# A jump-table hint on TensorE, and earlier loads, tables and drain, in an attention and mixture-of-experts kernel

## The chip, the cores and the metric

The kernel runs on one core of a Trainium2 chip. The core has five engines that work in parallel, each with an instruction stream of its own: TensorE (PE in the profile; its weight loads are listed as PEld), VectorE (DVE), ScalarE (ACT), GpSimd (POOL) and SyncE (SP), which here only issues DMAs. They wait for each other through semaphores. [...] The metric is the device time of one execution in microseconds, as a median over runs.

## The reference

All in float32: talking-heads attention, then a mixture of eight experts of which each token takes one.

```python
def _attn_ref(q, k, v, w_pre, w_post):          # 8 batches, 12 heads, 448 positions, 64 wide
    scores = scale * np.matmul(q, k.transpose(0, 1, 3, 2))
    scores = np.einsum('bhij,hg->bgij', scores, w_pre)
    scores = scores - np.max(scores, axis=-1, keepdims=True)
    attn = np.exp(scores)
    attn = attn / (np.sum(attn, axis=-1, keepdims=True) + 1e-09)
    attn = np.einsum('bhij,hg->bgij', attn, w_post)
    return np.matmul(attn, v)
...
def _moe_ref(x, w_gate, w1, w2):                # 3584 tokens of 768, 8 experts, hidden 1024
    ...
    expert_idx = np.argmax(logits, axis=1)
    ...
    for e in range(E):
        mask = expert_idx == e
        h = np.maximum(x[mask] @ w1[e], 0.0)
        out[mask] = gate_w[mask, None] * (h @ w2[e])
```

## The kernel before

**Attention** takes 32 query tiles (four to a batch: three of 120 queries and one of 88), and cuts each tile into *units* of 20 queries: six for a full tile, five for a short one, 184 in all. A hand-written schedule hangs steps on unit numbers, `at(u, priority, step, ...)`, and emits them unit by unit in order of priority; each engine then executes its own part in that order. The steps that matter here are these. `load_q` brings a tile's queries into `qr`, and `order_q` (POOL, L123) copies them in another order into `qq`, in two halves. `qk` (L238) makes the scores of one pair of heads, beginning QLEAD = 8 units ahead of the tile's own first unit, one pair per unit; a copy on ACT or DVE (L240) takes them out of PSUM, and a relayout DMA (L251) turns them into `sb`. Mixing over heads follows on PE (L265), the maximum on DVE, the exponential on ACT, the weights `wp` on POOL (L290), the second mixing and transposition on PE (L308), a copy `pt` on DVE (L319), and the product with `vt` on PE (L339). `load_k` and `load_v` bring the next batch's keys and values in chunks, and batch 0's values during the first units. At the very start PE warms up on matmuls whose result nobody uses (`heat`), VectorE clears the five `sb` tiles (L190), and small weights arrive through ScalarE's queue.

**Routing** is spread over the attention: for each tile `choose` finds the best expert, `weight` its gate, `count` its place in the expert's list by two small matmuls (L463, L466), and `dispatch` writes token number and gate into the DRAM table `TB` by an indirect DMA on POOL (L485); `store_x` writes the tile's rows into the DRAM array `XD`. The last two tiles (O and T in the code) have a `tail` list of their own that orders these steps by hand, with a long `heat` in it.

**Experts** come after that, one after the other. `load_t` reads 512 entries of an expert's table (L678), a copy `ti` and its clipped form `tcl` follow on DVE (L681, L682), and `load_x` gathers the rows in four slots of 128 tokens by indirect DMAs on POOL (L689). `turn_x` transposes them on PE (L706) and splits them into `xh` and `xl` (float32 precision is kept by splitting each operand into a high and a low part and adding three products). `hidden_of(e)` is a `tc.Switch` on `width[e]`, an entry of the small table `wide` that is known only at run time: it has six bodies, which compute the hidden layer for 352, 384, ... 512 tokens (L770 on PE); the Switch's own instructions are recorded on L951, and each body begins with a hint for the branch at its end (L781). `result(e, s)` makes one slot's output (L797 on PE, L802 on DVE, L804 on ACT, a scatter on POOL at L806); the fourth slot stands in a `tc.If` on the width (L834), since many experts have no more than 384 tokens. The weight chunks are fetched with SP as `wraw` (L519) and split on ACT and DVE (L526, L527). Every engine loads the eight widths into registers (L726). After the last expert a loop serves tokens that did not fit; with these inputs it is not entered, and the program ends with drains and semaphores, recorded on L951.

## Time and profile before

| | |
|---|---|
| time, median of 3 runs | 1334.51 us (1333.62 to 1341.18) |
| the profiled execution | 1335.38 us, span 1333.7 us |
| busy share of the span | PE 92%, VectorE 57%, ScalarE 49%, GpSimd 28% |
| granted TensorE clock, mean | 0.978 of full speed |
| experts begin (first L770 matmul) | 785.70 us |

The trace belongs to one execution; all times in it count from the start of its span. A row of the timeline gives start, length, engine, line, operation, and in brackets how long the engine had stood idle before it and what released it. The releaser is inferred. "issue" means that the profile shows nothing that the engine waited for. Names ending in q, such as PEldq or SPq, are an engine's sequencer or queue: branches, register loads, semaphores and DMA issues, which are not counted as busy. [...]

### The profile page before, as it was taken

To read this page: it belongs to the slowest core of one execution; us is meant where nothing else is said; L and a number is where in the kernel's file an instruction comes from. 1 tells how busy PE (TensorE), PEld (TensorE's weight loads), DVE (VectorE), ACT (ScalarE), POOL (GpSimd) and SP (SyncE) were. 2 spreads that over 40 slices of the span, in tenths; PEclk is the share of its full clock that TensorE was granted. 3 is DMA by queue.
4 is the path that set the end of the run, shared out by engine and by line. 5 is a ranking of instruction groups with operands and counts; after the bars stand their busy time and mean duration, and the time that the engine had idled before them with its cause. 6 is when DMAs were issued, how large, how long until landed. Compare 5 with 4: busy or idle time off the path is not lost. (4 is left out here: it accounts for less than half of the span.)

```text
span 1333.7 us, 54843 instructions
## 1 busy us (share of the span) xinstructions
PE 1223.8 (92%) x23808; PEld 1070.3 (80%) x23808; DVE 754.2 (57%) x1600; ACT 653.2 (49%) x1417; POOL 378.3 (28%) x921
## 2 busy tenths in 40 slices
PE   7789989999999899999999879899999999989995
PEld 3477878777777787877888779798989999979995
DVE  4567767777777677776878555252434243434320
ACT  3466766666666666766775334232323232323220
POOL 2234443435344434344443230101020202010000
PEclk9899999999999999999999979899999999989998
DMA  5655555656565646565645255343444444444210
GB/s 150 174 168 176 179 167 171 189 160 199 163 189 164 183 149 190 156 188 169 182 152 184 67 195 163 123 144 131 144 132 141 145 129 156 155 132 145 86 38 32
DMA packets 116293, 202.08 MB, mean 152 GB/s; under 512 B 40658, under 2 KB 90018, under 8 KB 115924
## 3 DMA queue, kind: packets, MB, share of 16 engines
q1 hardware_dynamic: 108398, 172.16, 42.2%
q0 software_dynamic: 6064, 23.86, 5.2%
q8 instruction: 212, 3.47, 1.1%
q10 hardware_dynamic: 1462, 1.30, 0.4%
q14 instruction: 157, 1.29, 0.3%
HBM read 97.59 MB, written 23.06 MB: 90 GB/s over the span
## 5 line engine op out<-in xcount | busy, mean ns | idle before, releaser
L265 PE MATMUL bm<-sb,Wpre 64*64 64x448 f32 x1440 | 319.5, 546 | 5.2 <-ACT et L277 3.1
L339 PEld LDWEIGHTS bx<-pt,vt 64*64 64x64 f32 x5856 | 282.9, 134 | 23.4 <-issue 11.6
L339 PE MATMUL bx<-pt,vt 64*64 64x120 f32 (+3 forms) x5856 | 290.8, 249 | 8.9 <-issue 4.9
L277 ACT ACTIVATE et<-bm,st 128x448 f32<-128x448 f32 (+1 forms) x368 | 233.0, 636 | 110.0 <-DVE st L271 102.8
L271 DVE TENSOR_REDUCE st<-bm 128x1 f32<-128x448 f32 (+1 forms) x368 | 223.0, 619 | 82.4 <-PE bm L265 65.4
L308 PE MATMUL bp<-wp,et 60*64 60x60 f32 x10080 | 225.5, 223 | 33.1 <-issue 27.3
L308 PEld LDWEIGHTS bp<-wp,et 60*64 60x64 f32 x10080 | 202.5, 136 | 46.6 <-issue 38.6
L319 DVE COPY pt<-bp 128x960 f32<-128x960 f32 (+1 forms) x184 | 215.7, 1172 | 38.8 <-PE bp L308 33.3
L240 ACT COPY si<-bs 120x896 f32<-120x896 f32 (+1 forms) x188 | 170.1, 905 | 102.2 <-PE bs L238 90.9
L238 PE MATMUL bs<-kr,qq 64*64 64x448 f32 x1504 | 194.5, 556 | 7.2 <-ACT si L240 6.9
L290 POOL TENSOR_SCALAR wp<-Wpost,st 128x60 f32<-128x60 f32 (+1 forms) x368 | 110.5, 312 | 239.5 <-DVE st L287 174.8
L265 PEld LDWEIGHTS bm<-sb,Wpre 64*64 64x64 f32 x1440 | 95.5, 135 | 78.9 <-issue 37.9
L770 PE MATMUL pm_h<-xh,ah 128*128 128x512 f32 (+4 forms) x384 | 145.1, 378 | 14.9 <-issue 9.7
L806 POOL DMA_INDIRECT out<-y,ti x30 | 30.9, 1029 | 443.8 <-ACT ah L526 135.7
L770 PE MATMUL pm_h<-xl,ah 128*128 128x512 f32 (+4 forms) x384 | 144.1, 375 | 0.0
L770 PE MATMUL pm_h<-xh,al 128*128 128x512 f32 (+4 forms) x384 | 143.8, 374 | 0.0
L774 DVE SCALAR_TENSOR_TENSOR hl<-pm_h,hh 128x512 fp32r<-128x512 f32 (+4 forms) x64 | 41.0, 641 | 165.5 <-ACT hh L773 164.4
L773 ACT ACTIVATE hh<-pm_h 128x512 fp32r<-128x512 f32 (+4 forms) x64 | 35.7, 558 | 184.5 <-PE pm_h L770 184.5
L797 PE MATMUL pm_y<-bh,hh 128*128 128x384 f32 x480 | 124.7, 341 | 0.0
L797 PE MATMUL pm_y<-bh,hl 128*128 128x384 f32 x480 | 122.3, 336 | 0.0
L797 PE MATMUL pm_y<-bl,hh 128*128 128x384 f32 x480 | 122.3, 336 | 0.0
L804 ACT ACTIVATE y<-pm_y,tb 128x384 f32<-128x384 f32 x30 | 17.4, 580 | 165.2 <-PE pm_y L797 88.2
(123 smaller groups left out, 1616.1 us busy)
## 6 DMA issues: line engine op xcount, KB each, us to landing
sb<-si SPq DMA_DIRECT2D x359, 210.0 KB
wraw<-in_w SPq DMA_DIRECT2D x64, 384.0 KB
wraw<-in_w SPq DMA_DIRECT2D x46, 512.0 KB
vt<-in_v SPq DMA_DIRECT2D x64, 192.0 KB
kr<-in_kT SPq DMA_DIRECT2D x48, 224.0 KB
qr<-in_qT SPq DMA_DIRECT2D x48, 180.0 KB
XD<-xr SPq DMA_DIRECT2D x24, 360.0 KB
qr<-in_qT SPq DMA_DIRECT2D x16, 132.0 KB
```

The lines of the kernel that those rows point to most:

```text
L238: nc.tensor.matmul(out=bank[cs, r, :S], lhsT=QQ[T][hs, c, cs], rhs=KR[b, c][hs, :], start=True, stop=True)
L240: copy(out=SI[T][:ni, 2 * c:2 * c + 2, :], in_=bank[:ni, :, :S])
L265: nc.tensor.matmul(out=bank_m[x][c * D:(c + 1) * D, :S], lhsT=Wpre[hs, :], rhs=SB[T, s][hs, c, :], start=True, stop=True)
L271: nc.vector.reduce_max(out=st[:top, 0, x:x + 1], in_=bank_m[x][:top, :S], axis=AX.X, negate=True)
L277: nc.scalar.activation(out=et[:top, x, :], in_=bank_m[x][:top, :S], func=AF.Exp, bias=st[:top, 0, x:x + 1], scale=1.0, accum_out=st[:top, ...
L290: nc.gpsimd.tensor_scalar(out=wp[:top, x, :], in0=Wpost[:top], scalar1=st[:top, 2, x:x + 1], scalar2=1.0, op0=ALU.mult, op1=ALU.mult)
L308: nc.tensor.matmul(out=bank_p[g * D:(g + 1) * D, n, o:o + nw], lhsT=et[hs, x, j * D:(j + 1) * D], rhs=wp[hs, x, :], start=True, stop=True)
L319: nc.vector.tensor_copy(out=to, in_=src[:, :2 * nh])
L339: nc.tensor.matmul(out=o, lhsT=VT[b % 2][ks, c, h * D:(h + 1) * D], rhs=i, start=(c == 0), stop=(c == NJ - 1))
L770: nc.tensor.matmul(out=ph[:, :n], lhsT=wx[:, fs], rhs=xx[:, kt, :n], start=(m == 0), stop=(m == 3 * NK1 - 1))
L774: nc.vector.scalar_tensor_tensor(out=hl[:, ft, :n], in0=ph[:, :n], scalar=0.0, in1=hh[:, ft, :n].bitcast(F32), op0=ALU.max, op1=ALU.subtract)
L797: nc.tensor.matmul(out=py[g][:, :384], lhsT=hx[:, kt, ts], rhs=wx[:, g * 384:(g + 1) * 384], start=(n == 0), stop=(n == 3 * NK2 - 1))
```

## The change

The change has five parts. (1) In slot 2 of every expert but the last, ahead of `result(e, 2)`, PE gets a jump-table hint: it loads the next expert's width and names the Switch body that this width selects; the Switch then knows of this hint. Only PE has it. (2) The five `sb` tiles are cleared before the small weights' tiles, not behind them. (3) `load_v` of batch 0 comes two units earlier, `load_k` of batch 1 later, and `order_q` one unit later for every tile from 2 on. (4) In the tail, tile O is weighed, counted and dispatched before the last tile's first half is taken; the second product of the last tile (`whole`) comes later; the warming is 66 long instead of 50, and 4 instead of 2 between the first expert's transposes. The widths are computed, and loaded, right behind the last dispatch, ahead of the weight splits, and the two fetches on ScalarE's queue come behind four splits. (5) In the last expert POOL drains before the conditional fourth slot.

```diff
@@
     heat(10, bank_m[0])
+    sbs = [sb_p.tile([P, 2, S], F32, name=f"sb{n}") for n in range(5)]
+    for t in sbs:
+        nc.vector.memset(t, 0.0)
     w12 = const.tile([P, 2, H], F32, name="w12")
...
-    sbs = [sb_p.tile([P, 2, S], F32, name=f"sb{n}") for n in range(5)]
-    for t in sbs:
-        nc.vector.memset(t, 0.0)
...
-                at(max(u0 - QLEAD - 2 + half, 1), 0.5 + 0.01 * T, order_q, T, half)
+                at(u0 - QLEAD - 1 + half, 0.5 + 0.01 * T, order_q, T, half)
         if it == 0 and b + 1 < B:
-            for c, k in enumerate((1, 3, 4, 8, 9, 12)):
+            for c, k in enumerate((1, 3, 4, 8, 9, 12) if b else (7, 8, 9, 10, 11, 13)):
                 at(u0 + k, 5.6, load_k, b + 1, c)
...
-                    (whole, T, 1, banks_s), (take_a, T, 0, bank_m), (take_b, T, 0, bank_m),
-                    (rows, T, (0, 1, 2), bank_x, 0), (weight, O), (store_x, O),
-                    (take_a, T, 1, banks_s), (take_b, T, 1, banks_s), (count, O),
-                    (rows, T, (3, 4, 5), bank_x, 3 * DW), (dispatch, O),
+                    (weight, O), (count, O), (dispatch, O), (take_a, T, 0, bank_m),
+                    (take_b, T, 0, bank_m), (whole, T, 1, banks_s),
+                    (rows, T, (0, 1, 2), bank_x, 0), (store_x, O),
+                    (take_a, T, 1, banks_s), (take_b, T, 1, banks_s),
+                    (rows, T, (3, 4, 5), bank_x, 3 * DW),
...
-                    (weight, T), (count, T), (heat, 50, bank_m[0]), (dispatch, T),
+                    (weight, T), (count, T), (heat, 66, bank_m[0]), (dispatch, T),
...
-        at(k, 5.65, load_v, 0, (k,))
+        at(max(k - 2, -1), 5.65, load_v, 0, (k,))
...
-        next_w(nc.scalar)
-        next_w(nc.scalar)
-        for n in range(2, NK1 - 1):
+        ...
+        width = [nc.values_load(wide[0:1, e:e + 1], min_val=0, max_val=len(WIDTHS) - 1,
+        ...
+        for n in range(RAWLEAD):
             split_w(n)
+        for n in range(2):
+            fetch_w(nc.scalar)
+        split_w(RAWLEAD)
...
-            heat(2, pm_h.tile([P, CAP], F32, name="pm_h"))
+            heat(4, pm_h.tile([P, CAP], F32, name="pm_h"))
...
+    HINT = {}
+
     def hidden_of(e):
         at0 = dict(turn)
-        for n in tc.Switch(width[e], len(WIDTHS)):
+        for n in tc.Switch(width[e], len(WIDTHS), hint=HINT.pop(e, None)):
...
                 if s == NS - 2:
+                    HINT[e + 1] = tc.switch_hint({mybir.EngineType.PE: width[e + 1]}, len(WIDTHS),
+                                                 label=f"wide{e + 1}")
+
                     def between():
...
             result(e, s, between)
+        if e == NE - 1:
+            nc.gpsimd.drain()
         with tc.If(width[e] > WIDTHS.index(SHORT)):
             result(e, NS - 1)
```

The order of PE's stream in expert 0, around the transposes (`pm_x<-ident,xs`) of slot 2; `pm_y` rows are matmuls of `result`. Before:

```order
L797 MATMUL pm_y<-bh_15672,hh 128x384 x2
L797 MATMUL pm_y<-bl_15673,hh 128x384 x2
L797 MATMUL pm_y<-bh_15672,hl 128x384 x2
L706 MATMUL pm_x<-ident,xs 128x128 x6
L797 MATMUL pm_y<-bh_15658,hh 128x384 x2
L797 MATMUL pm_y<-bl_15659,hh 128x384 x2
L797 MATMUL pm_y<-bh_15658,hl 128x384 x2
L797 MATMUL pm_y<-bh_15660,hh 128x384 x2
```

After, where line numbers from here on are those of the changed kernel (L797 has become L802, L706 has become L724):

```order
L802 MATMUL pm_y<-bl_15695,hh 128x384 x2
L802 MATMUL pm_y<-bh_15694,hl 128x384 x2
L724 MATMUL pm_x<-ident,xs 128x128 x6
L834 SWITCH_STRIDE
L669 TENSOR_LOAD wide
L834 ISA
L834 BRANCH_PREFETCH_HINT
L802 MATMUL pm_y<-bh_15680,hh 128x384 x2
L802 MATMUL pm_y<-bl_15681,hh 128x384 x2
L802 MATMUL pm_y<-bh_15680,hl 128x384 x2
L802 MATMUL pm_y<-bh_15682,hh 128x384 x2
```

Four instructions now stand between the transposes and the first matmuls of `result(0, 2)`; the branch that they concern is that of the next Switch, behind the rest of slot 2 and slot 3.

VectorE's stream at the start of the program (`w` and `warm` are the small weights' tile and the tile with which ScalarE warms up; `si<-bx` are the copies of scores). Before:

```order
L92 MEMSET bp 128x1024
L148 MEMSET w_132 128x24
L154 MEMSET warm 1x1
L178 MEMSET Wpre 128x64
L180 SCALAR_TENSOR_TENSOR Wpre<-w_132,mask 128x60
L184 TENSOR_TENSOR Wpost<-w_132,mask 128x60
L190 MEMSET sb_176 128x896
L190 MEMSET sb_177 128x896
L190 MEMSET sb_178 128x896
L190 MEMSET sb_179 128x896
L190 MEMSET sb_180 128x896
L240 COPY si<-bx 120x896 x4
```

After:

```order
L92 MEMSET bp 128x1024
L149 MEMSET sb_132 128x896
L149 MEMSET sb_133 128x896
L149 MEMSET sb_134 128x896
L149 MEMSET sb_135 128x896
L149 MEMSET sb_136 128x896
L151 MEMSET w_142 128x24
L157 MEMSET warm 1x1
L181 MEMSET Wpre 128x64
L183 SCALAR_TENSOR_TENSOR Wpre<-w_142,mask 128x60
L187 TENSOR_TENSOR Wpost<-w_142,mask 128x60
L240 COPY si<-bx 120x896 x4
```

The five clearings moved from between `Wpost` and the first copies to the front, ahead of the clearing of `w`.

SyncE's stream at the junction of attention and experts (`XD<-xr` are the last tiles' rows, `tb<-TB` the read of expert 0's and then expert 1's table). Before:

```order
L251 DMA sb_179<-si 120x1x448
L413 DMA XD<-xr 120x768 x3
L413 DMA XD<-xr 88x768
L726 TENSOR_LOAD wide x8
L678 DMA tb<-TB 128x4x2
L519 DMA wraw_14450<-in_w 128x768
L519 DMA wraw_14451<-in_w 128x768
L519 DMA wraw_14448<-in_w 128x768
L519 DMA wraw_14449<-in_w 128x768
L678 DMA tb<-TB 128x4x2
```

After:

```order
L251 DMA sb_135<-si 120x1x448
L413 DMA XD<-xr 120x768 x3
L413 DMA XD<-xr 88x768
L696 DMA tb<-TB 128x4x2
L520 DMA wraw_14451<-in_w 128x768
L520 DMA wraw_14452<-in_w 128x768
L520 DMA wraw_14449<-in_w 128x768
L520 DMA wraw_14450<-in_w 128x768
L696 DMA tb<-TB 128x4x2
L669 TENSOR_LOAD wide
```

The eight loads of widths ahead of the first read of the table are gone; one load stands behind the second read, ahead of the first Switch, and each later expert has its own.

## Rows read from the trace of the kernel before

**Rows 1.** The page's busy time by engine: busy us (share of the span), instructions.

```profile
PE 1223.8 (92%) x23808; PEld 1070.3 (80%) x23808; DVE 754.2 (57%) x1600; ACT 653.2 (49%) x1417; POOL 378.3 (28%) x921
```

**Rows 2.** The page's group of hidden matmuls, and the list of waits (total, times, longest).

```profile
L770 PE MATMUL pm_h<-xh,ah 128*128 128x512 f32 (+4 forms) x384 | 145.1, 378 | 14.9 <-issue 9.7
PE pm_h L770 <- issue: 9.7, 2, 4.9
PE pm_h L770 <- ACT y L804: 5.2, 5, 1.3
```

**Rows 3.** Line L951, where the Switch is recorded: PE's branches (ns min/median/max), all, then 905 to 914 us.

```profile
L951 PEldq COMPARE_BRANCH  x16: 321/438/4312, 783.6 to 1280.9; - x16
L951 PEldq COMPARE_BRANCH  x1: 3412/3412/3412, 911.0 to 911.0; - x1
```

**Rows 4.** Line L770 by stretch (us, PE busy, PEld busy, PEclk, DMA share, GB/s), and the chain.

```profile
840.00:900.00 60.00, 35.55 (x144) 28.73 (x144) 0.94 0.35 117
905.00:975.00 70.00, 33.24 (x144) 26.97 (x144) 1.00 0.42 136
1181.17 35.08 PE pm_h L770 x144
```

**Rows 5.** Timeline of the beginning: start us, us, engine, line, operation [idle before].

```profile
9.37 4.57 DVE L190 MEMSET sb<- 128x896 f32 x5
13.86 1.03 DVE L240 COPY si<-bx 120x896 f32<-120x896 f32 x1
14.99 1.76 PE L238 MATMUL bx<-kr,qq 64*64 64x448 f32 x8 [5.10 <-POOL qq L123]
```

**Rows 6.** Timeline of the first tiles, and two stretches (PEclk is the number behind POOL's).

```profile
34.94 0.80 POOL L123 COPY qq<-qr 128x360 f32<-128x360 f32 x1 [3.91 <-DMA qr<-in_qT]
37.46 1.10 PE L308 MATMUL bp<-wp,et 60*64 60x60 f32 x56 [2.85 <-DVE pt L319]
61.78 0.35 PE L339 MATMUL bx<-pt,vt 64*64 64x60 f32 x6 [3.47 <-DMA vt<-in_v]
38.00:42.00 4.00, 4.00 (x88) 2.33 (x82) 1.99 (x4) 2.09 (x5) 0.79 (x3) 0.57 0.26 91
62.00:66.00 4.00, 4.00 (x93) 3.47 (x90) 1.70 (x4) 1.45 (x4) 0.88 (x4) 0.57 0.05 18
```

**Rows 7.** The junction: timeline, register loads by line, and a stretch of both.

```profile
760.49 1.03 POOL L485 DMA_INDIRECT TB<-tg,di  x1 [2.74 <-DMA TB<-tg,di]
762.08 1.23 DVE L527 TENSOR_TENSOR al<-wraw,ah 128x1024 fp32r<-128x1024 f32 x1 [0.25 <-issue]
L726 SPq TENSOR_LOAD <-wide x8: 261/273/487, 763.6 to 766.1; - x8
770.04 0.17 DVE L681 COPY ti<-tb 128x4 int32<-128x4 int32 x1 [4.02 <-DMA tb<-TB]
776.12 1.51 PE L706 MATMUL pm_x<-ident,xs 128*128 128x128 f32 x6 [7.56 <-DMA xs<-XD,tcl]
785.70 0.46 PE L770 MATMUL pm_h<-xh,ah 128*128 128x352 f32 x1
772.00:786.00 14.00, 8.21 (x37) 7.84 (x38) 6.34 (x10) 3.35 (x7) 4.42 (x4) 0.51 0.66 227
```

**Rows 8.** The end: timeline of POOL, and POOL's drains on the program's last line.

```profile
1311.28 0.97 POOL L806 DMA_INDIRECT out<-y,ti  x1 [7.40 <-ACT y L804]
1319.60 0.98 POOL L806 DMA_INDIRECT out<-y,ti  x1 [7.34 <-DVEq _compat.py:109]
L951 POOLq DRAIN  x3: 40/112/7834, 1325.0 to 1333.4; - x3
```

**Rows 9.** POOL's waits for qr, the page's score matmuls, and tile 2's first eight of them.

```profile
POOL qq L123 <- DMA qr<-in_qT: 36.4, 16, 5.1
L238 PE MATMUL bs<-kr,qq 64*64 64x448 f32 x1504 | 194.5, 556 | 7.2 <-ACT si L240 6.9
42.29 0.96 PE L238 MATMUL bs<-kr,qq 64*64 64x448 f32 x8
```

## Prediction

> **What bounds the kernel now.** I read the page's table of busy time first: TensorE (PE) is busy for 92% of the span and nothing else passes 57% [rows 1]. So the end moves only where PE stands still, or where it runs at a lower clock. Four kinds of such places matter for this change, and I looked for each in the view that shows it.

> *The jump into an expert's hidden layer.* The page's group of L770 matmuls carries 14.9 us of idle time ahead of it, of which 9.7 is put down to "issue", that is to nothing the profile can name [rows 2]. The list of waits says that these 9.7 us are two waits, the longer 4.9 [rows 2]; the other 5.2 lie in five shorter ones, the longest 1.3 [rows 2]. The rows of the Switch itself name the cause: PE's COMPARE_BRANCH on L951 (Switch branches and body exits together, 16 of them) takes 321 ns at least, 438 ns in the middle, and up to 4312 ns [rows 3]; one ahead of a short stop took 3412 ns [rows 3]. In five experts PE still has matmuls queued while the branch is out, so only a quarter or so of it shows. In the two that follow a skipped fourth slot, PE's queue is empty first and all of it shows.

> *The clock after such a stop.* The 144 hidden matmuls of a 512-wide expert keep PE busy 33.24 us at a granted clock of 1.00, but 35.55 us from 840 on, behind the first long stop, at 0.94 in that stretch [rows 4], and 35.08 us from 1181.17 on, behind the second [rows 4]. The stops of about 1 us leave no such mark.

> *Beginning.* VectorE clears five sb tiles from 9.37 for 4.57 us, and only then makes the copy si<-bx at 13.86 that frees the bank for which PE idles 5.10 us, until 14.99 [rows 5]. The row names POOL as releaser, but POOL's copy is no later than VectorE's, and VectorE's is what stands behind the clearing.

> *Two stalls in the first tiles, the junction, the end.* PE idles 2.85 us before 37.46 and 3.47 before 61.78; ahead of the first, POOL stood for 3.91 us at its copy qq<-qr, for the DMA; the second waits for vt itself [rows 6]. After each the granted clock of 4 us is 0.57 [rows 6]. At the junction the last table entry is scattered at 760.49, VectorE has the read-back table at 770.04, and PE idles 7.56 us before its first transposes at 776.12; it starts hidden work at 785.70, at a clock of 0.51 over these 14 us [rows 7]. At the end the last scatter starts at 1319.60, and then a POOL DRAIN of up to 7.834 us, starting at the 1325.0 of the first of three, runs nearly to the end of the span [rows 8].

> **The parts and their costs.** The profiled execution took 1335.4 us (span 1333.7 and 1.7 outside), 0.9 more than the median of the three runs.

> *Hint on PE.* Added on PE for seven experts: a stride setting, one register load, one register operation and the hint. A load takes about 0.3 us here (273 ns in the middle on SyncE's row [rows 7]), the rest less. They stand among 0.34-us matmul pairs that are queued ahead of execution, and that queue hides them; with no cover they would cost some 0.5 us x 7 = 3.5. What they should remove: if the branch falls from 3.3-4.3 us to the 0.3-0.44 of the hinted exits, the five short stops go (5.2 us), and of the two long ones (9.7) about 1.0 us each stays, since there the queue is drained and the branch and its register work still follow. That is 12.9 us. The clock then stays up: 35.55 - 33.24 = 2.3 and 35.08 - 33.24 = 1.8, together 4.1. Full effect 17.0. Evidence that a hint on PE works at all: half of the 16 branches are exits of bodies of some 290 PE instructions that carry a hint at their head, and the middle of the 16 is 438 ns [rows 3]. But a hint's place is not free: it stands some 215 instructions before its branch, and I cannot show what happens if both lie in one block of fetched code. I count six of seven sites: **14.6 us** (bounds 0 and 17.0; a loss is a rival).

> *Beginning.* The five clearings now come before the small memsets, so VectorE's copy no longer stands behind them; instead ScalarE's issues and its warm-up come some 4.5 us later, because they wait for a memset behind the clearing. PE's 5.10 us stop could vanish, and ScalarE's first copies slip by about 3 us, which takes part of it back. **3 us** (bounds 0 and 5.1).

> *Early loads.* vt of batch 0 is issued two units earlier, the next batch's kr later, and POOL's copy qq<-qr one unit later, so POOL stands less in front of the weights wp that PE waits for. Prices of the two stalls: 2.85 + 3.47, plus a clock of 0.57 for 4 us twice, 0.43 x 4 x 2 = 3.4; together 9.8. The earlier vt shares the queue with the first relayouts, so I do not take all: **7 us** (bounds 0 and 9.8). Later tiles: POOL waits 36.4 us for qr in all, 16 times [rows 9]; PE's idle time after most of these is small, and I take nothing.

> *Junction.* The last but one tile's table entry goes out before the last tile's work instead of after it, so the last scatter needn't wait for it (it waited 2.74 us [rows 7]); SyncE's eight register loads from 763.6 to 766.1, ahead of its read of the table, are gone [rows 7]. But VectorE now does its eight loads and four weight splits before it looks at the table. Four splits of 1.2 us [rows 7] behind eight loads of 0.3, all behind the widths, which are ready near 759, give about 768.4 with the casts ahead of the first split, instead of 770.04: 1.6. The warming runs 66 long instead of 50, so PE should reach the transposes at a higher clock; what that saves of 776.12 to 785.70 is limited by the gathers. **2.5 us** (bounds -1 and 5).

> *Drain.* POOL drains before the last conditional, in slot 3's matmuls: slot 2's scatter starts 8.3 us before slot 3's [rows 8]. If the 7.83 us are work that has piled up and can be done early, the drain runs from 1312.3 to 1320.1, the last scatter is about 1 us late and the final drain short (the shortest DRAIN there takes 40 ns): 6.7 us saved. If it begins only as late behind the scatter as it did at the end (5.4 us), it delays the last scatter by some 5 us and saves 2.8. If it is a fixed price of the end, nothing is saved. I take **6 us**, nearer to the first.

> Sum: 14.6 + 3 + 7 + 2.5 + 6 = 33.1; 1335.4 - 33.1 = 1302.3, say 1302.

> **Rivals.** *The hint does nothing* (the fetch still begins only at the branch). For it: a one-shot hint through a register is in no row of before. Against: the hinted exits. Time 1302 + 14.6 = 1317. [...]

> *The drain cannot be brought forward*: 1308, or 1307 to 1311 with a late scatter. For it: no row shows a long drain anywhere but at the end.

> *The other side: score matmuls starved by order_q.* POOL's copy for tiles from 2 on moves one unit closer to the matmuls that read it. In tile 2, the tightest, the copy starts at 34.94 and lasts 0.80, and the tile's first score matmul starts at 42.29: 6.5 us [rows 6, 9]. A unit is near 3.8 us (188 groups of eight score matmuls over some 710 us [rows 9]), so 2.7 us remain. From the point where POOL comes 2.7 us later than now, each further us costs 1 us in each of 30 tiles; 1.6 us further is 48 us, which makes 1302 + 48 = 1350. Against: each tile has its own slack, and the longest wait of POOL for qr, 5.1 us [rows 9], shrinks with the move.

> **How the numbers follow.** Forecast with all parts 0.62; hint without effect 0.19 (1317); drain without effect, hint working 0.12 (1308); starved matmuls 0.03 (1350); other small failures together 0.04 (hint and drain both idle, 1323). With every part at its better bound the time would be 1335.4 - 17 - 5.1 - 9.8 - 5 - 6.7 = 1292; I cut this to 1293. On the upper side 1318 takes in the hint that does nothing. Outside are the double failure, the starved matmuls and the tails, under 0.2. A measurement of this kernel can tell about 1% from no change, which puts the bounds at 1321 and 1348. Faster than 1321 are all cases but the last two: 0.88; within 1% the double failure and weak tails, 0.09; slower 0.03.

> **What would show it.** Hint: PE's COMPARE_BRANCH on the Switch line with its maximum below 0.5 us, "issue" ahead of the hidden matmuls from 9.7 to about 2, and 33.2 us for 512-wide experts throughout. If the seven branches stay at 3.3-4.3 the hint failed. Beginning: the 5.10 gone, a stop of at most 2 in its place. Early loads: no stop over 2 us between 25 and 65. Junction: first transposes near 774, minus what came before. Drain: one long DRAIN before the last scatter, short ones at the end, and some 14 minus 6 us from the last matmul to the end. The forecast is wrong above all if hints on PE serve only branches with a fixed target, or if the drain waits for something that ends late anyway.

## The result, and the profile after

| | before | changed |
|---|---|---|
| median, first comparison (4 runs each) | 1337.85 us | 1303.68 us |
| ratio to before, 95% interval | | 0.968 (0.9624 to 0.9737) |
| ratio in a second comparison (6 runs against 11) | | 0.9747 (0.9707 to 0.9786) |
| profiled execution: span, mean granted clock | 1333.7 us, 0.978 | 1303.2 us, 0.995 |

The forecast was 1302. The ratios come from fast runs alone; the medians of the first comparison, which hold one slow run of the changed kernel, give 0.974, and so do those of the second. The span of the profiled pair can be cut at three instructions that both have: PE's last count matmul of routing (L463), the first hidden matmul of the experts (L770, now L773), and the end of the last matmul.

| stretch | before | changed | difference |
|---|---|---|---|
| start to the last count (attention) | 757.0 | 752.6 | -4.4 |
| last count to first hidden matmul (junction) | 28.7 | 27.2 | -1.5 |
| first hidden matmul to the last matmul (experts) | 532.6 | 515.1 | -17.5 |
| last matmul to the end (tail) | 15.4 | 8.3 | -7.1 |

The page's busy row and its clock row of the changed kernel:

```profile
PE 1216.5 (93%) x23852; PEld 1069.6 (82%) x23852; DVE 758.3 (58%) x1600; ACT 654.7 (50%) x1417; POOL 378.6 (29%) x921
PEclk9999999999999999999999999999999999999999
```

PE does the same work (44 matmuls more, all warming) and has fewer idle microseconds around it; no slice of the span lies below nine tenths of the clock. What answers to [rows 2, 3], PE's branches on the Switch line (now L961; ns min/median/max) and the page's group of hidden matmuls:

```profile
L961 PEldq COMPARE_BRANCH  x16: 321/418/3345, 776.6 to 1257.5; - x16
L961 PEldq COMPARE_BRANCH  x1: 2922/2922/2922, 776.6 to 776.6; - x1
L961 PEldq COMPARE_BRANCH  x1: 3345/3345/3345, 968.1 to 968.1; - x1
L961 PEldq COMPARE_BRANCH  x1: 1766/1766/1766, 1103.9 to 1103.9; - x1
L773 PE MATMUL pm_h<-xh,ah 128*128 128x512 f32 (+4 forms) x384 | 143.0, 372 | 5.6 <-issue 3.9
```

Of the seven hinted branches five take 0.32 to 0.34 us, that of expert 5 takes 1.77, that of expert 3 is as long as before. The eighth, of the first expert, has no hint; it took 0.35 us before and takes 2.92 now. The idle time ahead of the hidden matmuls fell from 14.9 to 5.6, and 2.92 of the 5.6 are the first expert's. What answers to [rows 4] (stretch, PE busy, PEld busy, clock, DMA share, GB/s), the two experts behind a skipped slot:

```profile
830.00:890.00 60.00, 33.24 (x144) 26.97 (x144) 1.00 0.45 143
1155.00:1200.00 45.00, 33.24 (x144) 26.97 (x144) 1.00 0.46 147
```

Both 512-wide hidden layers now take the 33.24 us that only the others took. At the beginning and in the first tiles, answering to [rows 5, 6]:

```profile
11.60 1.08 DVE L240 COPY si<-bx 120x896 f32<-120x896 f32 x1
12.22 0.98 PE L238 MATMUL bs<-kr,qq 64*64 64x448 f32 x8 [1.60 <-ACT si L240]
38.00:42.00 4.00, 3.04 (x98) 1.85 (x94) 2.87 (x6) 2.34 (x6) 0.80 (x3) 1.00 0.71 231
62.00:66.00 4.00, 4.00 (x142) 3.66 (x135) 3.27 (x6) 3.18 (x9) 1.74 (x5) 1.00 0.81 227
```

VectorE's copy comes 2.3 us earlier; PE's stop of 5.10 has become one of 1.60, for ScalarE's copy, which now waits for its late start (in the other runs with the early clearings it is longer, as told below). Both stretches that ran at 0.57 run at 1.00. At the junction, answering to [rows 7]:

```profile
754.44 1.03 POOL L485 DMA_INDIRECT TB<-tg,di  x1 [1.59 <-DVE wf L664]
758.69 4.63 DVE L528 TENSOR_TENSOR al<-wraw,ah 128x1024 fp32r<-128x1024 f32 x4 [0.50 <-DMA tb<-TB]
763.24 0.16 DVE L699 COPY ti<-tb 128x4 int32<-128x4 int32 x1
769.95 0.85 PE L724 MATMUL pm_x<-ident,xs 128*128 128x128 f32 x6 [2.24 <-DMA xs<-XD,tcl]
779.78 0.40 PE L773 MATMUL pm_h<-xh,ah 128*128 128x352 f32 x1 [2.92 <-issue]
767.00:780.00 13.00, 6.80 (x56) 6.11 (x55) 6.49 (x20) 3.45 (x8) 3.47 (x3) 1.00 0.54 180
```

The table is in VectorE's hands 10.7 us behind the last count instead of 13.1; the row shows that VectorE takes it the moment that its four splits end. The clock stays at 1.00. Then 2.92 us are lost ahead of the first hidden matmul. At the end, answering to [rows 8], two scatters and the drains (L843 is the new one, L961 the program's end):

```profile
1287.87 0.98 POOL L811 DMA_INDIRECT out<-y,ti  x1 [7.40 <-ACT y L809]
1297.60 0.98 POOL L811 DMA_INDIRECT out<-y,ti  x1 [8.75 <-issue]
L843 POOLq DRAIN  x1: 8968/8968/8968, 1287.7 to 1287.7; - x1
L961 POOLq DRAIN  x3: 46/113/140, 1301.2 to 1302.9; - x3
```

The record of the new drain begins under the scatter ahead of it (to 1288.85) and goes on for 7.8 us, the length of the drain at the end of before. The last three take 0.3 us together. The last scatter begins 2.8 us behind VectorE's part of `y` (1294.80) instead of 1.4.

### The profile page after: what moved, and what is told of

The parts are those of the page before. It is cut to its first block, busy times and chain, and to the rows that moved or that the text cites. A ratio compares the mean times of both kernels' runs of the same rounds, so it can differ in the third digit from the quotient of the medians.

```text
span 1303.2 us, 54974 instructions
## 1 busy us (share of the span) xinstructions
PE 1216.5 (93%) x23852; PEld 1069.6 (82%) x23852; DVE 758.3 (58%) x1600; ACT 654.7 (50%) x1417; POOL 378.6 (29%) x921
## 3 DMA queue, kind: packets, MB, share of 16 engines
q14 instruction: 155, 1.27, 0.3%
## 5 line engine op out<-in xcount | busy, mean ns | idle before, releaser
L238 PE MATMUL bs<-kr,qq 64*64 64x448 f32 (+1 forms) x1504 | 195.1, 547 | 13.2 <-ACT si L240 10.3
L773 PE MATMUL pm_h<-xh,ah 128*128 128x512 f32 (+4 forms) x384 | 143.0, 372 | 5.6 <-issue 3.9
L773 PE MATMUL pm_h<-xl,ah 128*128 128x512 f32 (+4 forms) x384 | 142.5, 371 | 0.0
L773 PE MATMUL pm_h<-xh,al 128*128 128x512 f32 (+4 forms) x384 | 142.0, 370 | 0.0
L802 PE MATMUL pm_y<-bh,hh 128*128 128x384 f32 x480 | 124.6, 341 | 0.0
L802 PE MATMUL pm_y<-bh,hl 128*128 128x384 f32 x480 | 122.4, 336 | 0.0
L802 PE MATMUL pm_y<-bl,hh 128*128 128x384 f32 x480 | 122.3, 336 | 0.0
L809 ACT ACTIVATE y<-pm_y,tb 128x384 f32<-128x384 f32 x30 | 17.5, 582 | 165.0 <-PE pm_y L802 81.1
```

Source lines behind the costliest of these rows:

```text
L238: nc.tensor.matmul(out=bank[cs, r, :S], lhsT=QQ[T][hs, c, cs], rhs=KR[b, c][hs, :], start=True, stop=True)
L773: nc.tensor.matmul(out=ph[:, :n], lhsT=wx[:, fs], rhs=xx[:, kt, :n], start=(m == 0), stop=(m == 3 * NK1 - 1))
L802: nc.tensor.matmul(out=py[g][:, :384], lhsT=hx[:, kt, ts], rhs=wx[:, g * 384:(g + 1) * 384], start=(n == 0), stop=(n == 3 * NK2 - 1))
```

## The experiments

**Without the hint.**

```diff
                 if s == NS - 2:
-                    HINT[e + 1] = tc.switch_hint({mybir.EngineType.PE: width[e + 1]}, len(WIDTHS),
-                                                 label=f"wide{e + 1}")
-
                     def between():
```

> The changed kernel without the hint; everything else as changed. If the hint is what shortened the experts, PE's seven Switch branches from the second expert on are back at 3.3 to 4.3 us, the two stops behind skipped slots at 4.8 to 4.9 us, the 512-wide experts behind them at 35 us instead of 33.2, and the stretch from the first to the last matmul of the experts is 16 to 18 us longer than in the changed kernel (515 us there, 532 before): about 1319 in all. Rival: the experts got shorter by the new order of weight fetches and register loads; then that stretch stays within 4 us of 515 and the time near 1304.

1328.97 us, ratio 0.9899 (0.9852 to 0.9946), clear of both intervals of the changed kernel. The experts take 534.2 us, 19.1 more than with the hint. The Switch line (here L958), the waits, the chain, and the hidden layer behind the first skipped slot by stretch:

```profile
L958 PEldq COMPARE_BRANCH  x16: 322/425/4897, 783.8 to 1281.4; - x16
PE pm_h L773 <- issue: 10.6, 2, 5.9
PE pm_h L773 <- ACT y L809: 7.0, 5, 1.6
1181.39 35.24 PE pm_h L773 x144
836.00:890.00 54.00, 34.81 (x144) 28.16 (x144) 0.97 0.37 117
```

All that [rows 2 to 4] show is back, the loss of clock somewhat smaller in the first of the two layers (34.81 us instead of 35.55), so the rival (that the new order of weight fetches shortened the experts) falls.

**The hint alone**, in the kernel before: `HINT` and the `hint=` of the Switch as in the change, nothing else.

```diff
-        for n in tc.Switch(width[e], len(WIDTHS)):
+        for n in tc.Switch(width[e], len(WIDTHS), hint=HINT.pop(e, None)):
...
+                    HINT[e + 1] = tc.switch_hint({mybir.EngineType.PE: width[e + 1]}, len(WIDTHS),
+                                                 label=f"wide{e + 1}")
```

> The kernel before with the hint alone. By the forecast's mechanism 13 to 17 us less than before (1318 to 1322 where before is 1335), all of it in the experts; the first matmul of the experts near 785.7 as before. One or two of the seven branches may stay long, where no boundary of fetched code lies between hint and branch. Rival: hint and the other parts only work together; then less than 6 us.

Ratio 0.9854 (0.9812 to 0.9896), 1319.81 us against 1337.5 on the same chip. The experts take 514.6 us, tail (15.7) and first matmul of the experts (788.6) are those of before, within the attention's spread. The Switch line (L956) and the group of hidden matmuls:

```profile
L956 PEldq COMPARE_BRANCH  x16: 321/416/2287, 787.6 to 1265.8; - x16
L770 PE MATMUL pm_h<-xh,ah 128*128 128x512 f32 (+4 forms) x384 | 142.5, 371 | 2.0 <-ACTq L839 2.0
```

The hint works by itself and for all but one branch (2.29 us, hidden by the queue). The 2.0 us left are the two stops behind skipped slots, 1.0 each as the forecast had them.

**Without the early drain.**

```diff
-        if e == NE - 1:
-            nc.gpsimd.drain()
```

> The changed kernel without the early POOL drain. If it was worth what it seems, the stretch from the last matmul to the end, 8.4 us in the changed kernel, is 15 us as before, with one DRAIN of 7.8 us behind the last scatter; the rest within noise. Rival: the end got shorter by the earlier semaphore work, and the stretch stays under 10 us.

The tail is 15.3 us, and the drain at the end (L959) is back:

```profile
L959 POOLq DRAIN  x3: 40/113/7834, 1293.6 to 1302.1; - x3
```

The time of this one run, 1304.05, is no longer than the changed kernel's, because its attention happened to end at 747.2 instead of 752.6. That is why the parts are told apart by stretches below, not by single times. Six more of the kernels below were executed once each, in 1294.8 to 1314.5 us.

**A drain in every expert, and one in the first alone.**

```diff
-        if e == NE - 1:
-            nc.gpsimd.drain()
+        nc.gpsimd.drain()
```

> POOL drains in every expert, not only in the last. If a drain's length follows the software DMAs issued since the last one (about 97 of them for 7.8 us, so 0.08 us each), the first drain takes some 3.5 us (44 DMAs), each later one about 0.6 us (8 DMAs), the one in the last expert is no longer than that, the last scatter is not late any more, and the end comes 2 to 3 us earlier behind the last matmul than in the changed kernel (8.4 us there). Rival: a drain with work behind it has a fixed price; then each of the eight takes about 7.8 us, and the last scatter is as late as in the changed kernel.

```diff
-        if e == NE - 1:
+        if e == 0:
             nc.gpsimd.drain()
```

> POOL drains only in the first expert, not in the last. If the long drain is work that piles up with each software DMA, the one in expert 0 covers about half of them and the one at the end the other half: about 4 us at the end, and a tail of 11 us behind the last matmul. Rival: the long part is due once, at the first drain of the program, whatever is behind it; then the last DRAIN takes 0.1 us, and the tail is near 7.

The eight drains of the first (L842, ns min/median/max), then both places of the second:

```profile
L842 POOLq DRAIN  x8: 3422/5502/7840, 830.6 to 1285.4; - x8
L843 POOLq DRAIN  x1: 7457/7457/7457, 839.9 to 839.9; - x1
L961 POOLq DRAIN  x3: 46/113/3897, 1308.0 to 1312.5; - x3
```

With the early one in expert 0 the drain at the end takes 3.90 us. 27 scatters and 20 gathers were issued between the two, 47 software DMAs; before, 7.83 us stood behind all 95 that the page lists. That is 0.08 us each in both (0.082 and 0.083), as if the work piled up; the one-time price falls. One figure doesn't fit the piling up. The first drain, with 48 software DMAs behind it, took 7.46 and 7.84 us in the two kernels, where 48 times 0.083 is 4.0; it began under the scatter ahead of it, by some 1.4 us, and ended 2.5 us behind the last packet of the software queue. Why it took so long stays open. In the other kernel neither expectation came: with some 8 software DMAs between drains I expected 0.6 us, a fixed price would be 7.8, and most took 3.4 to 6.1. The packets of the software queue suggest why: each of these drains from the second on ends 0.5 to 1.1 us behind the last of them, as if it also waited for transfers still under way. In the shade of the experts this costs nothing; the last scatter begins as early as before, and the tail is 6.8 us instead of 8.3.

**The hint one slot earlier, and PE's stream 64 instructions later.**

```diff
-                if s == NS - 2:
+                if s == NS - 3:
                     HINT[e + 1] = tc.switch_hint({mybir.EngineType.PE: width[e + 1]}, len(WIDTHS),
                                                  label=f"wide{e + 1}")
+                if s == NS - 2:
                     def between():
```

> The hint one slot earlier, some 300 instructions ahead of its branch instead of 207. If a hinted page is fetched when PE next passes a boundary of 256 instructions, and a hint without a boundary behind it is lost, then at least one boundary lies behind every hint now, and the branch of expert 3 (3.3 us in the changed kernel, boundary 246 instructions ahead of it, before the hint) falls to 0.35; that of expert 5 (1.8 us, boundaries 22 and 278 ahead) shows whether the page survives a second boundary: 0.35 if it does, 1.8 to 3.4 if not. Rival: what counts is the time between hint and branch, or nothing that depends on boundaries; then expert 3 stays at 3.3, or experts that were short become long at random.

```diff
-                    (weight, T), (count, T), (heat, 66, bank_m[0]), (dispatch, T),
+                    (weight, T), (count, T), (heat, 82, bank_m[0]), (dispatch, T),
```

> The changed kernel with 82 instead of 66 warming pairs, which puts 64 instructions more ahead of the experts on PE and changes nothing in them. By the boundary theory the long branches move: experts 3 and 5 become short (0.3 to 0.45), experts 1, 4 and 6, whose boundary then lies ahead of the hint, become long (3 to 5 us), and the first expert's own branch (2.9) becomes short. Rival: the long branch belongs to expert 3 for another reason (its width, its transfers); then it stays there.

```profile
L961 PEldq COMPARE_BRANCH  x1: 3336/3336/3336, 956.7 to 956.7; - x1
L961 PEldq COMPARE_BRANCH  x1: 630/630/630, 1093.2 to 1093.2; - x1
L961 PEldq COMPARE_BRANCH  x16: 316/378/440, 773.9 to 1252.0; - x16
```

Half of each expectation failed. In the shifted kernel experts 3 and 5 and the first expert became short as expected, but experts 1, 4 and 6 did too, though their boundary lies ahead of the hint. With the early hint expert 3 should have become short, since a packet was fetched 4.5 us behind the hint; it stayed at 3.34.

What the hinted branches agree with is narrower: the page that counts seems to be the one that holds the branch. Where it was entered, by that estimate, behind the hint and 60 or more instructions ahead of the branch (hint alone, experts 3, 4, 5 and 7: 60 to 210; changed kernel, experts 2, 4 and 7: 76 to 165), the branch took 0.32 to 0.42 us. Entered closer ahead it took up to 2.29 us. There the counts mislead, since they are read from the packets' times: eight profiled runs have the same stream ahead of expert 5's branch, and the same boundary comes out 22 to 46 instructions ahead of it. The times themselves say more. Expert 5's branch in these eight runs:

| last packet began ahead of the branch (us) | 0.60 | 0.62 | 1.54 | 1.75 | 1.89 | 2.11 | 2.31 | 2.57 |
|---|---|---|---|---|---|---|---|---|
| the branch took (us) | 1.77 | 1.76 | 1.21 | 1.27 | 1.15 | 0.44 | 0.42 | 0.44 |

With the early hint the pair is 2.01 and 0.63, and for expert 2 with the hint alone 0.12 and 2.29. So a branch that waited ended 2.3 to 3.0 us behind the start of its packet, and one whose packet began 2.1 us or more ahead was short. The first expert's branch, which has no hint, goes the same way (0.47 us behind the branch's start: 2.92; 2.2 ahead: 0.43). In the changed kernel's second profile (the last group of runs below) the first expert's branch and that of expert 5 are:

```profile
L961 PEldq COMPARE_BRANCH  x1: 1573/1573/1573, 778.0 to 778.0; - x1
L961 PEldq COMPARE_BRANCH  x1: 442/442/442, 1103.7 to 1103.7; - x1
```

The same two branches took 2.92 and 1.77 us in the first profile. The two experts behind a skipped slot, 1 and 6, took 0.32 to 0.43 us in all twelve profiles with the hint. Expert 3 took 3.32 to 3.69 us in all nine with the changed kernel's stream, the one with the early hint among them. Its boundary comes out 246 to 270 instructions ahead in these, so its branch may lie just behind the next boundary, where the page is entered too late; that reading isn't tested. Why a hint given behind the boundary worked for experts 1, 4 and 6 of the shifted kernel isn't settled either: for these a further packet was fetched between hint and branch, and for expert 3 of the changed kernel none was.

**The loads as before.**

```diff
-                at(u0 - QLEAD - 1 + half, 0.5 + 0.01 * T, order_q, T, half)
+                at(max(u0 - QLEAD - 2 + half, 1), 0.5 + 0.01 * T, order_q, T, half)
...
-            for c, k in enumerate((1, 3, 4, 8, 9, 12) if b else (7, 8, 9, 10, 11, 13)):
+            for c, k in enumerate((1, 3, 4, 8, 9, 12)):
...
-        at(max(k - 2, -1), 5.65, load_v, 0, (k,))
+        at(k, 5.65, load_v, 0, (k,))
```

> The changed kernel with load_v, load_k and order_q at their units of before (the whole of part 3 undone). If part 3 is what removed the two early stalls, both are back (near 3 us before the stage of 35, 3.4 behind the wait for vt near 58), the first score matmul of tile 3 comes near 66 to 68 us instead of 58, and the time is 4 to 8 us longer than the changed kernel's 1304 (part of the early gain is lost again by tile 7 in the changed kernel). Rival: the earlier loads only move the wait to the next batch's loads; then tile 3 is late but the count of the last tile and the time are the same within 2 us.

Both stops are back, at their places of [rows 6], and tile 3 begins at 69.4:

```profile
36.37 1.76 PE L308 MATMUL bp<-wp,et 60*64 60x60 f32 x56 [2.73 <-DVE pt L319]
62.08 0.49 PE L339 MATMUL bx<-pt,vt 64*64 64x60 f32 x6 [4.24 <-DMA vt<-in_v]
```

The two stops stand in all three profiles with the old loads and in none of the eleven with the new ones, so they are shown to come from the loads. What their absence is worth at the end is not resolved by the times: the six runs took 1298.2 to 1322.1 us (the profiled one 1320.24, its last count at 770.1), and the ratio, 0.978 (0.9686 to 0.9874), overlaps both comparisons of the changed kernel. Of the three edits only the sum was tried.

**The clearings where they were.**

```diff
-    sbs = [sb_p.tile([P, 2, S], F32, name=f"sb{n}") for n in range(5)]
-    for t in sbs:
-        nc.vector.memset(t, 0.0)
     w12 = const.tile([P, 2, H], F32, name="w12")
...
+    sbs = [sb_p.tile([P, 2, S], F32, name=f"sb{n}") for n in range(5)]
+    for t in sbs:
+        nc.vector.memset(t, 0.0)
     for part in range(2):
```

> The changed kernel with the five clearings of sb where they were before. By the forecast PE's stop of 5 us before 15 is back in place of the 1.6 to 4.3 us stop there, and the first score matmul of tile 1 comes near 19 to 20 us instead of 16.3 to 18.4; tile 3 near 60 to 61. Rival: the clearings are not what it waits for; then tile 1 stays at 16 to 18.4.

```profile
9.64 4.57 DVE L190 MEMSET sb<- 128x896 f32 x5
15.25 1.76 PE L238 MATMUL bx<-kr,qq 64*64 64x448 f32 x8 [5.70 <-POOL xt L194]
```

The stop is back, at 5.70 us where the runs with the early clearings have 1.60 to 4.45, and tile 1 begins at 19.8 instead of 17.5 (the middle of ten profiles with new loads and early clearings): 2.3 us. The named releaser is POOL, in this kernel another instruction of it than in [rows 5]; moving VectorE's work is what moved the stop.

**The tail's list in its old order.**

```diff
-                    (weight, O), (count, O), (dispatch, O), (take_a, T, 0, bank_m),
-                    (take_b, T, 0, bank_m), (whole, T, 1, banks_s),
-                    (rows, T, (0, 1, 2), bank_x, 0), (store_x, O),
-                    (take_a, T, 1, banks_s), (take_b, T, 1, banks_s),
-                    (rows, T, (3, 4, 5), bank_x, 3 * DW),
+                    (whole, T, 1, banks_s), (take_a, T, 0, bank_m), (take_b, T, 0, bank_m),
+                    (rows, T, (0, 1, 2), bank_x, 0), (weight, O), (store_x, O),
+                    (take_a, T, 1, banks_s), (take_b, T, 1, banks_s), (count, O),
+                    (rows, T, (3, 4, 5), bank_x, 3 * DW), (dispatch, O),
```

> The changed kernel with the tail's list in its old order (last but one tile dispatched after the last tile's halves; warming 66 as in the changed kernel). If the earlier dispatch is what brings the table earlier, the last scatter waits some 2.5 us for the one before it again, and from the last count to the experts' first matmul it takes 2 us longer than the 24 to 27 us seen with the new order. Rival: VectorE's loads and splits set the table's time anyway; then no difference beyond 1 us.

```profile
754.81 1.03 POOL L485 DMA_INDIRECT TB<-tg,di  x1 [2.80 <-DMA TB<-tg,di]
757.38 4.63 DVE L528 TENSOR_TENSOR al<-wraw,ah 128x1024 fp32r<-128x1024 f32 x4 [0.50 <-ACT ah L527]
761.92 0.16 DVE L698 COPY ti<-tb 128x4 int32<-128x4 int32 x1
```

The last scatter waits 2.80 us again and begins 3.6 us behind the last count (751.2) instead of 1.9. The table is used 10.7 us behind it all the same, right behind the splits, and the junction takes 25.1 us, within the 23.8 to 27.2 of the new order. The rival is right: the earlier dispatch is hidden by VectorE's loads and splits. SyncE issues the read of the table 5.9 us behind the last count here and 4.2 in the changed kernel, against 9.5 before, where its eight register loads stand ahead of it; removing these loads was not tried by itself.

**The changed kernel again, and a version with both gains.** The latter has 82 warming pairs and a drain in every expert (the two edits shown above).

> The changed kernel itself once more, as the measure for the others of this call. 1300 to 1306, ratio to before 0.965 to 0.976; experts 515 us, tail 8.3 us as in its first profile; what varies between executions is the attention, by some 6 us to either side.

> The changed kernel with 82 warming pairs (all seven hinted branches and the first one short) and with a drain in every expert (tail 6.8 instead of 8.3). First branch 2 us, branches of experts 3 and 5 hidden for the most part (0.8 us in the gaps), tail 1.5 us, minus what the longer warming costs at the junction: 2 to 5 us less than the changed kernel, if the two gains add. Rival: the attention's own spread hides it, and the shift costs as much at the junction as it gives: within 2 us.

1305.21 us, ratio 0.9747 (0.9707 to 0.9786), and 1302.13 us, ratio 0.972 (0.9683 to 0.9757). By stretch the second has what was expected: all eight branches at 0.32 to 0.43, junction 23.8 us against 26.4, tail 7.2 against 8.5. With 0.5 from the experts that makes 4.4 us, and the medians differ by 3.1; but the intervals of the two ratios overlap, so the times don't tell the two apart.

## Why the forecast was right

The mechanisms came as forecast but for one, the earlier dispatch in the tail. The sum came out to 2 us in part by luck: terms missed in both directions, the four stretches of the profiled pair add up to 30.5 us where 33.1 were forecast and the medians differ by 34.2, and the attention alone spreads over 20 us.

*Hint: 14.6 forecast, 17.5 measured* (the experts' stretch; 19.1 against the kernel without the hint). Six of seven sites at work was the right count, counting the late branch of expert 5 among them. The mis-sized step was to price the missing one as a seventh of 17.0. The site that failed, expert 3, follows a slot that was executed, so PE's queue hid most of the branch, and it cost 0.83. The two dear sites, behind skipped slots, worked; there the forecast's 1.0 of rest and the 4.1 us of clock are what was found. That makes 17.0 less 0.83, or 16.2. The 17.5 lies above even the full effect; the rest of 1.3 is no more than the 1.6 by which the stretch differs between the two kernels without the hint (532.6 and 534.2).

*Beginning: 3 forecast, about 2 measured.* The first score matmul of tile 1 moved from 19.2 to 17.5 in the middle of ten profiles. The slip of ScalarE's first copies was foreseen, and it is the stop of 1.60. But the sign named for it, a stop of at most 2, was met by that execution alone: in the ten other profiles with the early clearings PE stands 3.16 to 4.45 us there. The changed kernel's second profile has the longest, and a clock of 0.57 over 8 us:

```profile
12.21 1.02 PE L238 MATMUL bs<-kr,qq 64*64 64x448 f32 x4 [4.45 <-ACT si L240]
11.00:19.00 8.00, 6.79 (x40) 1.81 (x40) 2.87 (x4) 2.95 (x5) 5.02 (x14) 0.57 0.15 26
```

*Early loads: 7 forecast.* The first score matmuls of the tiles (each tile has 48, counted in order) and the last count, over the profiles. These kernels share the attention's program but for the loads and clearings (one has the tail's old order):

| begins at (us) | new loads and clearings, 10 profiles: lowest, middle, highest | old loads and clearings: before, hint alone |
|---|---|---|
| tile 1 | 16.3, 17.5, 18.4 | 19.2, 20.1 |
| tile 3 | 57.6, 58.6, 67.2 | 68.3, 69.2 |
| tile 7 | 147.1, 151.4, 159.9 | 158.3, 161.9 |
| last count | 742.8, 751.6, 763.1 | 757.0, 761.9 |

At tile 3 the two parts together have brought about 10 us, the forecast's 3 + 7. At the last count it is 5 to 10 by the middle, and 4.4 in the profiled pair; there the same attention differs by 20 us from one execution to the next, so nothing finer can be said. In the profiled pair 5.0 us were lost between tiles 3 and 7 (95.0 us against 90.0). The other nine profiles need 89.6 to 94.2 for that stretch and the two old ones 90.0 and 92.7, so most of the 5.0 belongs to that execution. What sets the spread was not tried by an experiment. The traces point at code fetches. The 67.2 at tile 3 is that of the kernel without the hint, which has the new loads: PE stood 2.54 us before 49.98 and 3.11 us before 58.55 there, for nothing that the profile names, and both times at an instruction whose number leaves 193 on division by 256.

```profile
58.55 0.63 PE L308 MATMUL bp<-wp,et 60*64 60x60 f32 x28 [3.11 <-issue]
```

A coarser count says less than it seems to: of the 55.1 us in which PE stood for over 0.3 us between 20 and 745 in the changed kernel, 49.0 belong to stops that touch the time from the start of a packet of its instruction queue to 1.5 us behind its end (47.7 of 52.3 before), but such times are 59% of the stretch.

*Junction: 2.5 forecast, 1.5 measured, for partly other reasons.* The table came 2.4 us earlier where 1.6 was forecast, and first transposes at 769.95 are what "near 774, minus what came before" said. The earlier dispatch, named as part of the reason, turned out to be worth nothing. The full clock shortened the transposes in the profiled pair (six took 1.51 us before and 0.85 after); in the changed kernel's second profile the clock from 767 to 780 was 0.87, so the longer warming doesn't secure it. And 1.5 is the difference of two executions: with the new order the junction took 23.8 to 27.2 us, and in the other kernel with the old one, the hint alone, 26.8. What I had not seen was that adding instructions ahead of the first Switch moves its own branch against the page boundaries. Counted from the start of the program, the last boundary lies 223 instructions ahead of the branch in before, at most 66 in the ten profiles with the changed kernel's stream, and 116 in the shifted kernel. The branch took 0.35 before and 2.92 in the profiled pair, but 0.43 to 1.57 in the other nine, by when the packet came, and 0.35 in the shifted kernel. So the missing term is 2.6 us in the profiled pair and some 0.7 in the middle of the others.

*Drain: 6 forecast, 7.1 measured.* The reading that work piles up holds at the end of the program (0.083 us per software DMA), the last scatter is 1.4 us late where 1 was forecast, and the drain began at once. The gain is above the better bound of 6.7, for the stretch from the start of the last scatter to the end fell by 8.5 us (14.1 to 5.6), and the forecast had counted the 7.8 of the drain alone.

Of the rivals, the hint without effect and the drain that can't be moved were each refuted by the run without them. Starved score matmuls did not show: the only wait of PE's score matmuls on POOL's copies in the changed kernel is one of 1.3 us, before 8 us.

## What to carry to other kernels

From the second expert on a Switch branch without a hint cost PE 3.35 to 4.90 us here, and a hint cut that to 0.32 to 0.44 where the last packet of code ahead of the branch began behind the hint and 2.1 us or more before the branch, with one exception (expert 3 with the early hint). 64 instructions added upstream moved these places (the first expert's branch went from 2.92 to 0.35 us, that of expert 3 from 3.35 to 0.33), and executions of one kernel differ (0.43 to 2.92 us for the first expert's branch in ten profiles of one stream), so look at each branch's duration again after any edit, in more than one profile. Price a miss by what the engine still has queued at that place: branches of 3 to 5 us cost 0.8 to 1.6 us where PE still had matmuls queued and 4.7 to 5.9, plus the lower clock behind it (0.94 over 60 us in before), where the queue had drained. Look at the end of the program for housekeeping that has piled up (a drain of 7.83 us behind 95 software DMAs here), and do it under the last matmuls (7.1 us less behind the last matmul); and where single times spread by more than a part is worth, cut the trace at instructions that both kernels have and compare stretch by stretch.

## What the runs showed of the hardware

- POOL's drain at the end of the program took about 0.083 us for each software DMA issued since the last drain (7.83 for 95, 3.90 for 47), though the software queue's last packet had ended 2.6 and 1.5 us before it began. Drains with 3 to 8 behind them took 3.42 to 6.14 us and ended 0.5 to 1.1 us behind the last packet of the software queue; the first drain in expert 0, with 48 behind it, took 7.46 and 7.84.
- A hint through a register on PE takes effect: branches of 3.35 to 4.90 us became 0.32 to 0.44. Where the packet that it waited for began less than 2.1 us ahead, a hinted branch took up to 2.29, and at expert 3 the hint did nothing in the changed kernel's stream (3.32 to 3.69).
- The first expert's branch, unhinted and to the first of the six bodies, took 0.43 to 2.92 us in ten profiles with the same stream, 2.92 where the packet of code began 0.47 us behind the branch's start and 0.43 where it began 2.2 us or more ahead.
- The granted clock fell behind some stops of about 3 us and not behind others: it was 0.57 over the 4 us behind stops of 2.85 and 3.47 us [rows 6], and 1.00 from 779.8 to 788 in the changed kernel, behind the stop of 2.92 us.
